# A fused attention, gating and rotation kernel: two weight transfers staged in another buffer, and one batch's attention handed out later

## The chip, the cores and the metric

The kernel runs on one core of a Trainium2 chip. The metric is the device time of the whole program in microseconds (us), as the median of several runs. TensorE (PE) does the matrix products, VectorE (DVE), ScalarE (ACT) and GpSimd (POOL) do the elementwise work, and SyncE (SP) issues nearly all DMA transfers.

## The reference, cut to what matters

```python
# B=4 batches, 8 heads, S=576 positions, 64 per head; 4 heads local (window 32), 4 strided (32)
attn = softmax(mask(q @ k.T / 8)) @ v          # heads joined: x is (B, 576, 512)
h = relu(x @ w_in)                             # 512 -> 1024
u, v = h[..., :512], h[..., 512:]
v_n = (v - mean(v)) / sqrt(var(v) + 1e-6)
v_s = einsum('ts,bsd->btd', w_spatial, v_n) + b_spatial[None, :, None]
x = (u * v_s) @ w_out
theta = x @ w_theta
y = einsum(w_tok_r, x * cos(theta)) + einsum(w_tok_i, x * sin(theta))
u2 = x + y
out = u2 + relu(u2 @ w_ch)
```

## The kernel before, in words

Every large matrix is held as two f16 halves, a high and a low part, and every product is three f16 passes (`PASS`: high x high, low x high, high x low). A weight therefore is loaded into a staging buffer, converted to its high part by ACT and to its low part by DVE or POOL, and only then read by PE. The weights `w_in`, `w_out`, `w_th`, `w_tr`, `w_ti` and `w_ch` come as 64-bit words and need four steps for each 128x1024 part: a load and two ACT activations (`a` and `b` in the hand-written list), a DVE operation (`c`), and the split into halves (`e`, ACT and POOL). The spatial weights `wsp` come as f32 and need one ACT activation and one DVE operation of 128x1152 for each of their two large parts (`sp_part(0)`, `sp_part(2)`); a third piece, `sp_tail`, holds the last rows and the bias.

There are two staging buffers, `raw0` (in tile `x2f`) and `raw1` (in tile `zf`), used in turn by `stage()`: a load into one waits until the conversion of what it held is done.

Batch 0's attention runs by itself at the start, in groups of blocks `s` = 0 to 11 (`attention0`; NG is 9). The lists in its call say what else is put between the groups: `l0`..`l3` are loads of `w_in`, `a`, `b`, `c`, `e` with the same number their conversion steps, `go` a piece of batch 0's first product with `w_in` (the half that makes v: `main_v(0)`, four times `go`), and `step` one step of batch 1's attention. Up to `pinned.clear()` each engine keeps the instructions in the order in which they are written. Batch 0's groups are written as: output transposes of group s-3 with their two evacuations into `xT[0]` (ACT high half, DVE low half), turns of group s-1, the product with V of group s-2.

After that come, for each batch, `main_v` (v), `main_mid` (u chunks, spatial chunks `sp`, products `x`, angles `th`) and `main_end` (`y` and `c`). Their instructions are no longer pinned; the tile framework's planner puts each engine's stream in order beforehand, by priorities and its own cost estimates, and at run time every engine follows its stream strictly. A count of matmul columns (`clock[0]/2400`, "clock" below, in us of TensorE at full speed) tells when to hand out other work: conversions (`conv`, by `timed(due, lead, gap)`), and steps of the next batch's attention, step n at `ATT_AT[b][0] + n*ATT_AT[b][1]`. `not_before` keeps a step's first score matmul behind the matmul that stood 3 us (`LEAD`) earlier on that clock. Since work is handed out only between chunks, a step falls on the next chunk's end.

Batch 1's attention (`attention1`) has a first step that only loads, and ten more, s = 0 to 9: scores and softmax of quad s, the transposes (`turn`) of quad s-1, the product with V (`px`) of quad s-2, whose results go to `xT[1]`. `xT[1]` is at first the place of batch 0's q and k of head pairs 2 and 3.

The names of matmul results in the profile: `at`, `sc`, `av` (banks of batch 0's groups; `av` and `sc` are also the turns and V products of batch 1), `a` (scores of batch 1), `v`, `u`, `sp`, `x`, `th`, `y`, `c`. `x2h` there is also the place of the converted 64-bit words (steps `b` and `c`), `sm` and `st` batch 1's softmax. Nearly all instructions stand on L107, the line of the helper that issues them.

Of the kernel before, what the change touches and what calls it, by code (L numbers as in the profile page):

```python
# [14 lines left out]
F32 = mybir.dt.float32  # L15
# [38 lines left out]
E_ZLO = 'vvvvvvvv'  # L54
WARM = 6
LEAD = 3.0
ATT_AT = (None, (2.7, 4.2), (86.0, 5.4), (174.5, 4.6))
PREP_AT = (112.0, 126.0, 131.0)
CONV_SP = (20.0, 9.9, 1.9)
CONV_OUT = (37.0, 12.0, 5.0)  # L60
# [9 lines left out]
def kernel(  # L70
# [52 lines left out]
    nc = Engines  # L123
# [17 lines left out]
    B, DM, S = out.shape  # L141
    P = 128
    NC = DM // P
    NF = S // P
# [61 lines left out]
    xT = [const.tile([P, 2, NC, S], F16, name=f"xT{i}") for i in range(2)]  # L206
# [10 lines left out]
    def s2(name):  # L217
        return scr.tile([P, 2, HS * 2], F32, tag="s2", name=name, bufs=4)
# [28 lines left out]
    def stage(late_raw=None):  # L247
        i = early[1]
        early[1] += 1
        if early[0]:  # L250
            return (raw0, raw1)[i % 2], vals[i % 2]
        return late_raw, s2("wx").rearrange("p a n -> p (a n)")
# [21 lines left out]
    def pair(ap, n):  # L274
        return ap[:, 0:2 * n].rearrange("p (a n) -> p a n", a=2)
# [12 lines left out]
    def prep_w(dst, src, c, i, late):  # L288
        for f in steps_w(dst, src, c, i, late):
            f()  # L290

    def win_steps(half, i):

        c = slice(half * DM, (half + 1) * DM)
        steps = []

        def load():
            steps.extend(steps_w(win, w_in, c, i, False, load_w(w_in, c, i)))

        return [load] + [lambda k=k: steps[k]() for k in range(4)]  # L300

    def sq_parts(dst, src, late=1):
        for i in range(0, NC, 2):
            yield lambda i=i: prep_w(dst, src, slice(0, DM), i, late)

    def sp_part(i):
        stg = pair(stage()[0].bitcast(F32), S)
        nc.sync.dma_start(stg, w_spT[i * P:(i + 2) * P, :].rearrange("(a p) n -> p a n", p=P))
        nc.scalar.activation(wsp[:, 0, i:i + 2, :], stg, AF.Copy, scale=SPS)
        nc.vector.scalar_tensor_tensor(wsp[:, 1, i:i + 2, :], stg, SPS, wsp[:, 0, i:i + 2, :],  # L310
                                       op0=ALU.mult, op1=ALU.subtract)
# [144 lines left out]
    NG = len(groups)  # L456
# [779 lines left out]
    def timed(parts, due, lead, gap):  # L1236
        parts = list(parts)
        for i, f in enumerate(parts):
            conv.append((due - lead - gap * (len(parts) - 1 - i), f))

    timed([lambda i=i: sp_part(i) for i in range(0, NF, 2)] + [sp_tail], *CONV_SP)
    timed(sq_parts(wout, w_out), *CONV_OUT)
    timed(sq_parts(wth, w_th), *CONV_TH)
    conv.append((conv[-1][0], switch))
# [10 lines left out]
    for at, f in [(at, lambda n=n: tok_load(*toks[n])) for n, at in enumerate(TOK_AT)] + [  # L1255
            (at, lambda: next(atts[N32])) for at in PREP_AT]:
        i = next((i for i, c in enumerate(conv) if c[0] > at), len(conv))
# [3 lines left out]
    def now():  # L1261
        return clock[0] / 2400.0

    def step():
        if next(atts[att["b"]], "end") == "end":
            att["b"] += 1
            att["n"] = 0
            return False
        att["n"] += 1
        return True  # L1270

    def others():
        while conv and conv[0][0] <= now():
            conv.pop(0)[1]()
        while att["b"] < B and ATT_AT[att["b"]][0] + att["n"] * ATT_AT[att["b"]][1] <= now():
            step()
# [13 lines left out]
    l1, a1, b1, c1, e1 = win_steps(1, 2)  # L1290
    l2, a2, b2, c2, e2 = win_steps(0, 0)
    l3, a3, b3, c3, e3 = win_steps(0, 2)
    v0 = main_v(0)

    def go():
# [6 lines left out]
        5: ((), (e0, l2)),  # L1302
        6: ((), (a1, b1)),
        7: ((), (c1, step)),
        8: ((), (e1, l3, go)),
        NG: ((), (go, step)),
        NG + 1: ((), (go, a2, b2, c2)),
        NG + 2: ((), (go, e2, a3, b3, c3, e3)),
    })
    pinned.clear()  # L1310
    run_main(v0)
# [93 lines left out]
```

## Time and profile before

| | |
|---|---|
| median of 3 runs | 489.07 us (488.37 to 489.84) |
| the profiled execution | 488.06 us, span 486.3 us |
| PE busy | 468.4 us, 96% of the span |
| DVE, ACT, POOL busy | 300.8, 267.2, 71.4 us |
[...]

The profiled execution's own time holds 1.8 us around its span. "Busy" of an engine is the time covered by its instructions; for PE the ends are modelled, so short gaps do not show.

### The profile page before, as it was taken

Reading aid. Unit: us, or ns where it says so; the run is one execution under the profiler, and the core shown is the slowest. Engines: PE = TensorE matmul, PEld = TensorE weight load, DVE = VectorE, ACT = ScalarE, POOL = GpSimd, SP = SyncE. Lnnn points to the kernel's source line nnn. Section 1 sums busy time; section 2 is a strip of 40 time slices with the busy share of each in tenths; the row PEclk is TensorE's granted clock in tenths of the full one; section 3 lists DMA queues with packets and bytes.
Section 4 is the critical chain, followed back from the end, with each engine's and each line's share of the span. In section 5 each row is a group of like instructions: output and inputs, shape, how many; then the busy total and the mean of one; then the engine's idle time right before and its main releaser. Section 6 shows DMA issues by size and latency. Waiting matters only on the chain. (4 is left out here: it accounts for less than half of the span.)

```text
span 486.3 us, 10776 instructions
## 1 busy us (share of the span) xinstructions
PE 468.4 (96%) x4440; PEld 352.3 (72%) x4440; DVE 300.8 (62%) x642; ACT 267.2 (55%) x470; POOL 71.4 (15%) x68
## 2 busy tenths in 40 slices
PE   7889889899999999999999999999999999999996
PEld 5665667676577778777568777777567777777775
DVE  3766998966998546752787878762686121227412
ACT  2657788879954334445945667754942022149202
POOL 2041124120015100201005100111005200210320
PEclk9999999999999999999999999999999999999999
DMA  6887666638760245100381345320450020003502
GB/s 179 288 243 208 201 224 217 195 154 245 161 148 1 69 163 148 54 0 1 86 217 52 91 123 158 67 44 1 74 122 1 2 98 0 1 2 76 121 0 99
DMA packets 71820, 52.72 MB, mean 108 GB/s; under 512 B 50584, under 2 KB 59992, under 8 KB 71770
## 3 DMA queue, kind: packets, MB, share of 16 engines
q1 hardware_dynamic: 71466, 51.42, 38.3%
q8 instruction: 35, 0.57, 0.5%
q10 hardware_dynamic: 304, 0.61, 0.4%
q14 instruction: 15, 0.12, 0.1%
HBM read 35.36 MB, written 4.72 MB: 82 GB/s over the span
## 5 line engine op out<-in xcount | busy, mean ns | idle before, releaser
L107 PE MATMUL y<-wtok,zf 128*128 128x288 f16 x864 | 107.2, 286 | 0.0
L107 PEld LDWEIGHTS <-zf 128*128 128x128 f16 x864 | 84.1, 98 | 22.2 <-issue 1.2
L107 PE MATMUL sp<-wsp,vn 128*128 128x288 f16 x384 | 50.3, 286 | 0.8 <-ACT u L107 0.8
L107 PE MATMUL x<-zf,wout 128*128 128x288 f16 x384 | 49.6, 287 | 0.0
L107 PE MATMUL u<-xT,win 128*128 128x288 f16 x384 | 49.3, 286 | 0.0
L107 PE MATMUL v<-win,xT 128*128 128x512 f16 (+1 forms) x240 | 48.4, 380 | 0.8 <-DVE xT L107 0.6
L107 PEld LDWEIGHTS <-vn 128*128 128x128 f16 x416 | 40.3, 98 | 11.2 <-issue 0.9
L107 PE MATMUL th<-x2h,wth 128*128 128x288 f16 x384 | 47.9, 286 | 0.3 <-DVE ta L107 0.3
L107 POOL TENSOR_TENSOR x2h<-x2f,x2h 128x576 f16<-128x576 f32 x19 | 26.6, 1403 | 142.7 <-issue 66.7
L107 PE MATMUL c<-x2h,wch 128*128 128x288 f16 x360 | 45.2, 286 | 0.0
L107 PEld LDWEIGHTS <-wth 128*128 128x128 f16 x384 | 37.6, 98 | 10.0 <-issue 0.5
L107 PEld LDWEIGHTS <-wch 128*128 128x128 f16 x384 | 37.4, 98 | 9.3
L107 PEld LDWEIGHTS <-win 128*128 128x128 f16 x384 | 37.4, 98 | 9.2
L107 PEld LDWEIGHTS <-wout 128*128 128x128 f16 x384 | 36.7, 98 | 9.5
L107 PEld LDWEIGHTS <-xT 128*128 128x128 f16 (+1 forms) x240 | 21.0, 100 | 25.3 <-issue 2.2
L107 ACT ACTIVATE x2h<-x2f 128x576 f16<-128x576 f32 (+1 forms) x28 | 20.9, 748 | 24.0 <-DVE x2f L107 23.5
L107 ACT ACTIVATE o<-c 128x576 f32<-128x576 f32 x15 | 9.7, 645 | 34.9 <-PE c L107 34.7
L107 DVE TENSOR_TENSOR ta<-ta,x2f 128x1152 f32<-128x1152 f32 (+1 forms) x17 | 21.7, 1284 | 11.2 <-ACT ta L107 11.2
L107 DVE SCALAR_TENSOR_TENSOR x2f<-y,x2f 128x576 f32<-128x576 f32 x16 | 12.1, 754 | 25.1 <-PE y L107 25.0
L107 DVE SCALAR_TENSOR_TENSOR o<-x2f,o 128x576 f32<-128x576 f32 (+1 forms) x17 | 12.2, 722 | 23.6 <-ACT o L107 23.6
L107 POOL TENSOR_TENSOR zf<-u,zf 128x576 f16<-128x576 f32 x8 | 10.2, 1277 | 112.9 <-ACT zf L107 112.9
L107 DVE TENSOR_TENSOR u<-u,sp 128x576 f32<-128x576 f32 x16 | 12.0, 750 | 22.4 <-PE sp L107 22.4
(146 smaller groups left out, 723.7 us busy)
## 6 DMA issues: line engine op xcount, KB each, us to landing
out_dram<-o SPq DMA_DIRECT2D x15, 288.0 KB
kt<-in_qp_dram SPq DMA_DIRECT2D x8, 288.0 KB
qs<-in_qd_dram SPq DMA_DIRECT2D x8, 288.0 KB
x2f<-in_w_in_dram SPq DMA_DIRECT2D x2, 1024.0 KB
zf<-in_w_in_dram SPq DMA_DIRECT2D x2, 1024.0 KB
xT<-in_w_ch_dram SPq DMA_DIRECT2D x2, 1024.0 KB
kt<-in_kzl_dram SPq DMA_DIRECT2D x8, 152.0 KB
ks<-in_kl_dram SPq DMA_DIRECT2D x4, 304.0 KB
```

Source lines behind the costliest of these rows:

```text
L107: ins = f(*args, **kwargs)
```

## The change

The two large parts of the spatial weights get a staging place of their own, the whole of `xT[1]` seen as f32. Their loads are issued with the last `w_in` load (`l3`), at group 8, and their conversions are put in the pinned list at the end of batch 0's attention, around the last `w_in` conversion; only `sp_tail` stays in `conv`. The first three conversion steps of the u half of `w_in` move one group earlier each. The second attention step of batch 1 moves from group 9 to the end of the list, and the further ones are handed out from clock 5.7 every 4.4 instead of 2.7 every 4.2. With two fewer uses of `stage()`, `sp_tail` and `w_out` still alternate as before.

```diff
-ATT_AT = (None, (2.7, 4.2), (86.0, 5.4), (174.5, 4.6))
+ATT_AT = (None, (5.7, 4.4), (86.0, 5.4), (174.5, 4.6))
...
+    raw_sp = xT[1].rearrange("p e c n -> p (e c n)").bitcast(F32)
+
+    def sp_place(i):
+        return raw_sp[:, i * S:(i + 2) * S].rearrange("p (a n) -> p a n", a=2)
+
+    def sp_load(i):
+        nc.sync.dma_start(sp_place(i), w_spT[i * P:(i + 2) * P, :].rearrange("(a p) n -> p a n", p=P))
+
     def sp_part(i):
-        stg = pair(stage()[0].bitcast(F32), S)
-        nc.sync.dma_start(stg, w_spT[i * P:(i + 2) * P, :].rearrange("(a p) n -> p a n", p=P))
+        stg = sp_place(i)
...
-    timed([lambda i=i: sp_part(i) for i in range(0, NF, 2)] + [sp_tail], *CONV_SP)
+    timed([sp_tail], *CONV_SP)
...
-        8: ((), (e1, l3, go)),
-        NG: ((), (go, step)),
-        NG + 1: ((), (go, a2, b2, c2)),
-        NG + 2: ((), (go, e2, a3, b3, c3, e3)),
+        8: ((), (e1, l3, lambda: sp_load(0), lambda: sp_load(2), go)),
+        NG: ((), (go, a2, b2, c2)),
+        NG + 1: ((), (go, e2, a3, b3)),
+        NG + 2: ((), (go, c3, lambda: sp_part(0), e3, step, lambda: sp_part(2))),
```

## Rows read from the trace of the kernel before

**Rows 1.** The page, busy time, share of the span, instructions.
```profile
PE 468.4 (96%) x4440; PEld 352.3 (72%) x4440; DVE 300.8 (62%) x642; ACT 267.2 (55%) x470; POOL 71.4 (15%) x68
```

**Rows 2.** Windows: stretch, length; busy (count) of PE, PEld, DVE, ACT, POOL; clock; DMA.
```profile
30.00:57.00 27.00, 26.14 (x260) 16.33 (x258) 19.78 (x57) 17.76 (x27) 9.60 (x9) 1.00 0.76 212
57.00:80.00 23.00, 19.47 (x230) 14.62 (x231) 22.74 (x52) 19.98 (x30) 6.36 (x6) 1.00 0.71 232
80.00:100.00 20.00, 17.46 (x230) 13.11 (x228) 17.99 (x31) 17.05 (x24) 6.63 (x6) 1.00 0.69 232
100.00:125.00 25.00, 24.68 (x219) 17.36 (x218) 15.80 (x22) 21.81 (x32) 0.00 (x0) 1.00 0.59 163
...
46.00:63.40 17.40, 15.12 (x166) 11.09 (x166) 17.24 (x51) 14.50 (x21) 2.36 (x3) 1.00 0.52 161
```

**Rows 3.** PE's waits from 0 to 100 us: total, times, longest.
```profile
PE av L107 <- DVE sm L107: 3.6, 5, 1.0
```

**Rows 4.** PE's timeline: start, length, operation, count, idle time before and its releaser.
```profile
36.01 0.73 PE L107 MATMUL a<-kt 64*64 64x96 f32 x16
...
36.85 0.51 PE L107 MATMUL av<-ident,smx 128*128 128x128 f32 x3
...
37.95 4.06 PE L107 MATMUL v<-win,xT 128*128 128x512 f16 x18
...
42.07 5.46 PE L107 MATMUL v<-win,xT 128*128 128x512 f16 x30
...
48.57 6.04 PE L107 MATMUL u<-xT,win 128*128 128x288 f16 x48
...
58.49 0.61 PE L107 MATMUL av<-ident,sm 128*96 128x128 f32 x4 [1.52 <-ACT wspt L107]
...
62.34 1.63 PE L107 MATMUL sp<-wsp,vn 128*128 128x288 f16 x12 [0.76 <-ACT u L107]
```

**Rows 5.** DVE's timeline, single operations of the stretches that the steps touch.
```profile
45.81 1.35 DVE L107 SCALAR_TENSOR_TENSOR x2h<-zf,x2h 128x1024 int32<-128x1024 int32 x1 [2.78 <-DMA x2f<-in_w_spT_dram]
...
50.63 1.48 DVE L107 SCALAR_TENSOR_TENSOR wsp<-x2f,wsp 128x1152 f16<-128x1152 f32 x1
...
52.77 1.34 DVE L107 SCALAR_TENSOR_TENSOR wsp<-zf,wsp 128x1152 f16<-128x1152 f32 x1
...
57.79 0.55 DVE L107 TENSOR_TENSOR sm<-sm,st 128x384 f32<-128x384 f32 x1
...
61.05 2.36 DVE L107 TENSOR_TENSOR vn<-vr,vn 128x1024 f16<-128x1024 f32 x2
...
84.85 0.69 DVE L107 TENSOR_TENSOR sm<-sm,st 128x512 f32<-128x512 f32 x1
...
97.48 1.29 DVE L107 TENSOR_TENSOR sm<-sm,st 128x512 f32<-128x512 f32 x1
```

**Rows 6.** ACT's timeline around the last conversions of the input weights.
```profile
38.23 0.52 ACT L107 ACTIVATE sm<-sm 128x384 f32<-128x384 f32 x1 [3.33 <-DVE sm L107]
...
42.27 0.35 ACT L107 ACTIVATE xT<-at 128x216 f16<-128x216 f32 x1 [1.13 <-PE at L107]
...
43.63 1.13 ACT L107 ACTIVATE zf<-zf 128x1024 f32<-128x1024 f32 x1
44.65 1.13 ACT L107 ACTIVATE x2h<-zf 128x1024 int32<-128x1024 uint8 x1
```

**Rows 7.** SP's timeline: when DMA transfers are issued.
```profile
33.76 0.39 SPq L107 DMA_DIRECT2D zf<-in_w_in_dram  x1
...
36.96 2.54 SPq L107 DMA_DIRECT2D v<-in_vl_dram  x4
```

**Rows 8.** SP's waits from 39.0 to 42.6 us: total, times, longest.
```profile
SPq L107 <- DMA zf<-in_w_in_dram: 1.7, 1, 1.7
```

**Rows 9.** Windows, DVE's instructions on `st` alone: the first quad's softmax.
```profile
36.90:40.30 3.40, 2.52 (x6) 1.00 1.02 341
```

**Rows 10.** POOL's timeline, one low half of an angle weight.
```profile
97.04 2.76 POOL L107 TENSOR_TENSOR wth<-x2h,wth 128x512 f16<-128x512 f32 x2 [9.88 <-ACT wth L107]
```

## Prediction

> **What bounds the kernel now.** I read the page's busy times first. PE is busy 468.4 us of 486.3 [rows 1], so a change pays only where PE stands idle, and the question is which idle time this one can reach. It starts at about 35 us, when the last groups of batch 0's attention are written; whatever comes before is the same instructions on the same engines. The windows give PE's idle time after that: from 57 to 80 us 23.00 - 19.47 = 3.53 us, from 80 to 100 us 2.54 us, from 100 to 125 us 0.32 us [rows 2]. From 36 to 57 us PE has no recorded gap. That is 6.4 us in all, 1.3% of the time, and the most that can be won.
>
> The same rows name the cause. From 46 to 63.4 us DVE is busy 17.24 of 17.40 us, from 57 to 80 us 22.74 of 23.00, while after 100 us it is busy only 63% [rows 2]. Most of PE's waits are turns of batch 1's attention that stand behind DVE's softmax (3.6 us in five waits [rows 3]), and two more are of the same kind: 1.52 us before a turn at 58.49 and 0.76 us before the first spatial product at 62.34 [rows 4]. The ACT operations named as releasers there only came at the same time: the turn reads `sm`, which DVE divided until 57.79 + 0.55 = 58.34 us, and the low half of `vn`, which the spatial product reads, was half done at 61.05 + 1.18 = 62.23 us [rows 5]. So PE waits for a DVE queue, and what counts is how much DVE work stands ahead of each thing that PE needs.
>
> **The spatial weights.** The conversions are not removed: two ACT operations and two on DVE (1.48 + 1.34 = 2.8 us [rows 5]) are moved. Before, DVE did them at 50.63 and 52.77 and was through at 54.1, eight us ahead of the first spatial product at 62.34 [rows 4, 5]. PE never waited for them, so having the weights earlier is worth nothing in itself; their worth is a place in DVE's queue that was empty. There is such a place: DVE sat idle 2.78 us before the last `c` step at 45.81 [rows 5]. (The row names a DMA; the step reads what ACT's `b3` wrote, and that ended at 44.65 + 1.13 = 45.78 [rows 6].) The loads cost SP two issues of some 0.4 us [rows 7] and DMA time behind `l3`; the loads that they delay are those of batch 1's second head pair, first read some 20 us later. I cost both at nothing; without that cover they would add up to 2 us to a quad's scores.
>
> **The step of attention moved away from group 9.** Its scores take PE from 36.01 to 36.85 us, 0.85 us [rows 4], its softmax 2.52 us of DVE [rows 9]; ACT stood idle 3.33 us for it before 38.23 [rows 6]. Without it, `a2`, `b2`, `c2` run at about 35 to 38 us and `e2` to 39.4. That sounds like a head start of 4 us for `c3`, but it is not: `a3` reads the last `w_in` part, and this load lands late. SP had issued everything by 36.96 + 2.54 = 39.50 and then waited 1.7 us for just this transfer, so it landed at 41.2 us, 7.4 us after its issue at 33.76 [rows 7, 8]. Nothing ahead of it in SP's stream changes. Before, `a3` started at 43.63 [rows 6], so this gains 2.4 us at most.
>
> **What is queued behind `a3`.** The new list writes `a3` and `b3` one group earlier, ahead of the evacuation of the last attention group (`xT`, 0.35 us on ACT, at 42.27 before [rows 6]). ACT keeps the written order, so that copy now waits for the landing at 41.2 plus the two activations, 1.02 us apart and 1.13 long [rows 6]: 41.2 + 1.02 + 1.02 = 43.25, done at 43.6, DVE's low half at 44.0. PE, with the scores gone from its stream, gets to that point 0.85 us sooner: transposes done at 42.07 - 0.85 = 41.2, then the six matmuls of the fourth `go` at 4.06/18 = 0.226 us each [rows 4], so it is through at 42.5 us. What follows (chunk 3 of v, and the scores of quad 0, whose bank the same copy has to free) needs that copy. PE stands from 42.5 to 43.65 and once more before the low half: **a new stall of 1.3 us** (0 if the load lands by 39, 1.6 if the copy loses another place). This is the first term: +1.3.
>
> [...] If ACT could reorder, the term would be 0 and the forecast 1.3 us lower.
>
> **The first spatial product.** DVE's work from the last `c` step (45.81) to the normalisation that makes `vn` is the same, with quad 0's softmax in the place of quad 1's, but starts at 44.0, behind the low half of the late copy, 1.8 us sooner; I give 0.4 back for its wait on quad 0's exponential (0.52 us on ACT [rows 6]). If quad 1's softmax, whose scores now come after the first u chunk, stays behind `vn`, the low half of `vn` is ready at 62.23 - 1.4 = 60.8 us; if it is put ahead of it, as its softmax was before, 2.5 us more: 63.3. PE starts u at about 49.2 instead of 48.57: 44.0, then the rest of v (5.46 - 1.36 = 4.1 us) and quad 0's scores, about 1.1 with their start. It has u chunks 0 to 2 (72 products at 6.04/48 = 0.126 us, 9.1 us) and two quads' scores and turns (0.85 and about 0.6 each, 2.9 us [rows 4]) before it, so arrives near 61. The stall there is 0 or about 2.2 us against 1.52 + 0.76 = 2.3 before. I take the second as nearer to the order of before, with some allowance: -0.3 (from +1.0 to -2.3).
>
> **The later turns.** Batch 1's steps come one chunk later: counted on the clock, the scores of quad k stand where those of k + 1 stood (handed out at 16.6, 19.4, 25.6, 29.0, 32.4, 37.9, 41.5, 47.3, 51.6 instead of 13.8, 16.6, 22.8, 25.6, 29.0, 32.4, 37.9, 40.8, 47.3). At any point after 63 us DVE has 2.5 us less work behind it in the queue. The stalls there were 3.53 - 2.3 + 2.54 = 3.8 us [rows 2]. Some are of the moment, a softmax behind a conversion of 1.2 to 1.4 us, and stay. The last step moves to where DVE has room. I take half: -1.9 (0 to -3.0).
>
> **The stretch after 100 us.** The work put off is added to ACT's 21.81 us busy of 25 [rows 2], where ACT also works out the angles. The stall of 0.32 us there may double: +0.3 (0 to +1.0).
>
> Sum: +1.3 - 0.3 - 1.9 + 0.3 = -0.6 us. On the profiled execution's own time of 488.06 that gives 487.5; the median shown is 1.0 us above that execution, so 488.5.
>
> **A price beside it.** DVE's multiply of 128x512 took 0.69 us alone and 1.29 us while POOL worked on a low half at 97.04 [rows 5, 10]. POOL's part of `e3` moves to about 46.4 to 48.7 us, under the spatial conversion and quad 0's multiply, so up to 2 x 0.6 = 1.2 us of the DVE queue is at risk; it lies within the bounds of the `vn` term. [...]
>
> **The rivals.** *Faster:* the DVE queue really is the bound, quad 1's softmax falls behind `vn`, and most later turns find their input. Then +1.3 - 2.2 - 2.6 + 0.3 = -3.2, 485.9 us. For it speak DVE's 99% from 46 to 80 us [rows 2]; against it the late load, which leaves DVE idle from about 40 to 43.6 us in place of the 2.78 us saved. Chance 0.34. *Slower:* both softmaxes stand ahead of `vn`. This decides as soon as `vn`'s low half comes later than about 63.5 us; then PE loses 1.3 in front, 0.9 there, keeps its later stalls and gets 0.5 after 100 us: +2.7, 491.8 us. For it speaks that DVE was already late there by 2.3 us. Chance 0.24. *The change does nothing:* the weights were ready in time anyway, and the landing sets the pace before and after, with the new stall taken back by the old: within 0.5 us of 489.07. Chance 0.06.
>
> **How the numbers follow.** My forecast, a small gain of one term over the others, has 0.36. Within 0.3% (1.5 us, about what a measurement of this kernel can tell from no change) lie the forecast and the last rival: 0.42. Faster by more 0.34, slower by more 0.24. The range reaches to both outer cases, 485.3 to 491.5; the forecast's own is 487.4 to 489.9.
>
> **What would show it.** ACT's `a3` on `zf` near 41.2 us with idle time before it; PE idle for about 1.3 us near 42.5 us, with ACT's or DVE's `xT` as releaser; the spatial conversions on DVE between 45 and 51.5 us; u from about 49.2; the spatial product at 61 to 63; fewer and shorter waits of `av` on `sm` from 63 to 100 us. Wrong would be a landing well before 41 us, no gap at 42.5, or waits from 57 to 100 us as long as before.

## The result and the profile after

The changed kernel takes 493.15 us (median of six, 492.08 to 494.6) against 488.75 us for the kernel before, measured beside it. The ratio is 1.0069 with an interval of 1.0051 to 1.0088, a loss of some 3.4 us; the two medians lie 4.4 us apart. A second set of runs of the same kernel (`after_again`, below) gave 493.04 against 488.81. The forecast of 488.5, no change to speak of, was wrong, and 493.15 lies above its range. It is also above the rival that spoke of a loss (491.8).

The page of the changed kernel, busy times and the rows of the 40 slices for PE and its granted clock:

```profile
PE 471.7 (96%) x4440; PEld 354.5 (72%) x4440; DVE 302.5 (61%) x642; ACT 267.2 (54%) x470; POOL 71.7 (15%) x68
...
PE   7789979799999999999999999999999999999996
...
PEclk9999989899999999999999999999999999999999
```

PE has the same 4440 matmuls as before [rows 1] and is busy 3.3 us longer. That is the first thing to see: PE does not wait 3.3 us more, its work takes longer. The second is in the last row: the granted clock, full in the whole span of the profiled execution before, is lower in two slices, the sixth and the eighth. The same row of the kernel before:

```profile
PEclk9999999999999999999999999999999999999999
```

To take out whatever the two executions do differently before the change, I compare the stretch from PE's first v product to its first y product. Behind it nothing differs: from y to the end it is 355.2 us before and 355.5 after. (Ahead of it the profiled execution of the changed kernel is 2.5 us later than that of the kernel before, 33.85 against 31.35, because an early load of `w_in` landed late: ACT's step on it stood idle 1.59 us and began at 18.99 instead of 16.46; in `after_again` it is 1.1 us later. The change touches nothing there, and I leave it out.) The windows of that stretch, columns as in [rows 2], first the kernel before and then the changed one:

```profile
31.35:131.09 99.74, 93.04 (x941) 63.23 (x940) 81.00 (x163) 81.90 (x117) 21.24 (x19) 1.00 0.70 205
```

```profile
33.85:137.22 103.37, 96.13 (x940) 65.15 (x939) 83.48 (x165) 84.63 (x121) 22.27 (x19) 0.97 0.66 203
```

The stretch is 3.63 us longer. PE's idle time in it went from 99.74 - 93.04 = 6.70 us to 103.37 - 96.13 = 7.24, only 0.54 more. The mean clock went from 1.00 to 0.97. Windows of a quarter of a microsecond show how: the clock is 0.50 from about 64.8 to 68.2 us and from 95.5 to 98.9, and 1.00 in the rest of the stretch. In `wait_long` (below) PE does 25 matmuls in 6 us at a clock of 0.51 and 51 at 1.00. By that each of the two stretches costs up to half its length, 1.7 us, and both up to 3.41 us. PE still stands idle in the first 0.59 and 0.29 us of them, where a low clock costs nothing; without half of that, 0.44 us, the clock costs 2.97 us, and 0.54 + 2.97 = 3.51 us stands against the 3.63 measured. The windows around the two, changed kernel:

```profile
61.00:64.00 3.00, 1.34 (x28) 0.67 (x26) 3.00 (x6) 3.00 (x4) 0.00 (x0) 1.00 0.57 172
64.00:69.00 5.00, 3.99 (x28) 2.42 (x23) 5.00 (x13) 2.90 (x5) 2.95 (x2) 0.66 0.76 260
69.00:92.00 23.00, 22.41 (x246) 17.17 (x244) 19.60 (x34) 19.50 (x28) 11.08 (x9) 1.00 0.53 192
92.00:95.00 3.00, 1.31 (x42) 0.94 (x42) 2.97 (x7) 1.89 (x3) 0.00 (x0) 1.00 0.88 207
95.00:100.00 5.00, 4.22 (x23) 3.17 (x24) 4.24 (x9) 1.72 (x4) 0.00 (x0) 0.66 0.96 349
```

Both times there is a window in which PE is busy less than half of the time (1.34 and 1.31 of 3.00 us), and behind it one with the clock at 0.66 in the mean. Between them, from 69 to 92 us, PE is busy 22.41 of 23.00 us at full clock, 97%, where before it was 85 and 87% in the stretches from 57 to 100 us [rows 2]. PE's timeline names the waits, columns as in [rows 4]:

```profile
63.00 0.42 PE L107 MATMUL sp<-wsp,vn 128*128 128x288 f16 x2 [1.55 <-ACT vn L107]
63.53 0.56 PE L107 MATMUL a<-kt 64*64 64x96 f32 x16
...
65.36 3.01 PE L107 MATMUL sp<-wsp,vn 128*128 128x288 f16 x12 [0.99 <-DVE vn L107]
...
95.78 1.09 PE L107 MATMUL av<-ident,sm 128*128 128x128 f32 x4 [2.47 <-DVE sm L107]
96.66 4.21 PE L107 MATMUL x<-zf,wout 128*128 128x288 f16 x24
```

At the first place PE waits 1.55 us for `vn`, does two spatial products and a quad's scores, and waits 0.99 us more; in that second wait the clock falls. The twelve spatial products behind it take 3.01 us, twelve took 1.63 us before [rows 4]. At the second place a turn waits 2.47 us for its softmax, the clock falls 2.2 us into the wait, and the four transposes behind it take 1.09 us (0.63 in `late_handout`, whose clock falls after them). PE's waits as a whole, 33 to 130 us, columns as in [rows 3]:

```profile
PE av L107 <- DVE sm L107: 2.5, 1, 2.5
PE sp L107 <- ACT vn L107: 1.5, 1, 1.5
PE sp L107 <- DVE vn L107: 1.1, 2, 1.0
```

Against 3.6 us in five waits of at most 1.0 before [rows 3] it is one of 2.5. The waits became fewer, as forecast, but longer, and behind the long ones PE runs at half its clock.

### The profile page after: what moved, and what is told of

It is laid out like the page before. It is cut to its first block, busy times and chain, and to the rows that moved or that the text cites. A ratio compares the mean times of both kernels' runs of the same rounds, so it can differ in the third digit from the quotient of the medians.

```text
span 492.7 us, 10773 instructions
## 1 busy us (share of the span) xinstructions
PE 471.7 (96%) x4440; PEld 354.5 (72%) x4440; DVE 302.5 (61%) x642; ACT 267.2 (54%) x470; POOL 71.7 (15%) x68
## 5 line engine op out<-in xcount | busy, mean ns | idle before, releaser
L107 PE MATMUL sp<-wsp,vn 128*128 128x288 f16 x384 | 51.5, 291 | 2.5 <-ACT vn L107 1.5
L107 PEld LDWEIGHTS <-wout 128*128 128x128 f16 x384 | 37.7, 99 | 10.7 <-issue 0.6
```

The source lines that it names most:

```text
L107: ins = f(*args, **kwargs)
```

## The experiments

The theory: idle time is much the same in both kernels, and what costs is that it is gathered into a few long waits, behind which the granted clock falls for some 3.4 us. The rivals: a cost in the change itself (the early conversions, DVE's `c` of `w_out` ahead of `vn`, the queue behind `a3`), or more waiting in all. The table has all kernels, each beside its own runs of the kernel before (488.75 to 490.28 us in the median). "v to y" is the length of the stretch above less 99.74, "idle" PE's idle time in it less 6.70, both from one profiled execution; "clock" is the sum over quarter-microsecond windows of (1 - granted clock) x length, by the same reckoning the most that the low clock can cost.

| kernel | median us | ratio (95%) | v to y | idle | clock |
|---|---|---|---|---|---|
| the changed kernel | 493.15 | 1.0069 (1.0051 to 1.0088) | +3.63 | +0.54 | 3.41 |
| after_again | 493.04 | 1.0090 (1.0072 to 1.0107) | +3.31 | +0.38 | 3.41 |
| only_attention | 493.31 | 1.0094 (1.0072 to 1.0116) | +4.39 | +1.31 | 3.41 |
| only_staging | 494.60 | 1.0108 (1.0088 to 1.0127) | +5.21 | +3.53 | 1.71 |
| staging_again | 494.78 | 1.0119 (1.0080 to 1.0159) | +6.05 | +4.12 | 1.71 |
| early_steps | 488.86 | 0.9994 (0.9978 to 1.0010) | +0.72 | +0.46 | 0 |
| earlier_steps | 493.38 | 1.0081 (1.0052 to 1.0110) | +6.07 | +1.38 | 3.41 |
| start_only | 492.50 | 1.0063 (1.0041 to 1.0084) | +1.48 | -0.63 | 1.71 |
| gap_only | 491.51 | 1.0050 (1.0032 to 1.0068) | +1.66 | +0.43 | 0 |
| late_handout | 491.38 | 1.0043 (1.0024 to 1.0063) | +4.05 | +2.09 | 1.71 |
| wout_behind_vn | 494.97 | 1.0100 (1.0064 to 1.0136) | +7.19 | +4.75 | 1.71 |
| staging_split_first | 492.59 | 1.0037 (1.0012 to 1.0063) | +4.60 | +3.02 | 1.71 |
| split_again | 492.30 | 1.0061 (1.0039 to 1.0082) | +3.59 | +2.39 | 1.71 |
| filled_first | 495.74 | 1.0123 (1.0095 to 1.0151) | +6.49 | +1.02 | 3.41 |
| filled_both | 498.95 | 1.0198 (1.0173 to 1.0222) | +6.99 | +0.42 | 1.71 |
| wait_long | 501.91 | 1.0238 (1.0202 to 1.0275) | +0.39 | +0.66 | 0 |
| wait_short | 498.83 | 1.0169 (1.0134 to 1.0203) | +0.29 | +0.55 | 0 |

Idle and clock together give "v to y" within 0.75 us except in gap_only (1.2 us short), earlier_steps (1.3 us short) and the two filled kernels, which have added work. In the last two kernels the edit lies behind this stretch. What the two columns leave over is not explained.

**The same kernel again**

> The changed kernel once more, nothing edited. Two theories of its loss. Clock: in the first trace of the changed kernel TensorE stood idle twice in front of the first spatial product (1.55 and 0.99 us) and once at a turn near 95 us (2.47 us), and its granted clock fell to 0.5 for some 4 us behind each; the waits and the half clock together make the loss. If so, the second trace shows the low clock at the same two places, and a time of about 493 us. Queue: the copy of the last attention group stands behind the two activations that wait for the last input weights, and TensorE loses 1.3 us there. If so, a gap of about 1.3 us stands near 42.5 us after the start in this trace, which the first one may have hidden, since its first part was 2.5 us late from a slow transfer near 19 us.

The two low stretches stand behind the same two waits (1.54 + 0.99 us and 2.47 us). So the low clock of the changed kernel is not an accident of one execution. The mean clock of each of its twelve executions says the same: it is 0.982 to 0.993, and none is at 1.000. The kernel before is not free of low clock either. Of its 71 executions beside the experiments, 30 have a mean clock of 1.000 (median 489.10 us) and 11 one of 0.986 to 0.993 (median 490.75 us); the full clock of its profile is the most frequent case, not a rule. Such a mean is over the whole span and does not say where the clock fell: seven of the eighteen traces have a fall that starts near 8 us, ahead of all that the change touches, and by their mean clocks lose 1.7 us or more besides what the table's last column has.

**The two halves of the change**

`only_attention`, on the kernel before: the step behind the list, and the later, wider handing out.

```diff
-        NG: ((), (go, step)),
+        NG: ((), (go,)),
...
-        NG + 2: ((), (go, e2, a3, b3, c3, e3)),
+        NG + 2: ((), (go, e2, a3, b3, c3, e3, step)),
```

> The kernel before with the attention part alone: the second attention step of batch 1 moves behind the last conversion of the input weights, and the further steps are handed out from 5.7 every 4.4; the spatial weights are staged as before. Clock theory: the attention step that is taken away is what TensorE had to do while vn was made, so this alone opens the wait before the first spatial product; 491 to 494 us, with a granted clock below 1.0 near 65 us. Queue theory: nothing stands behind the last input weights that did not before, so no loss in front; 487 to 489.5 us.

`only_staging`, on the changed kernel: handing out as before, the weights still staged early.

```diff
-ATT_AT = (None, (5.7, 4.4), (86.0, 5.4), (174.5, 4.6))
+ATT_AT = (None, (2.7, 4.2), (86.0, 5.4), (174.5, 4.6))
...
-        NG: ((), (go, a2, b2, c2)),
-        NG + 1: ((), (go, e2, a3, b3)),
-        NG + 2: ((), (go, c3, lambda: sp_part(0), e3, step, lambda: sp_part(2))),
+        NG: ((), (go, step)),
+        NG + 1: ((), (go, a2, b2, c2)),
+        NG + 2: ((), (go, e2, a3, b3, c3, lambda: sp_part(0), e3, lambda: sp_part(2))),
```

> The changed kernel with its attention put back: the lists as before and steps from 2.7 every 4.2, and only the spatial weights loaded into the second xT and converted beside the last input weights. Clock theory: TensorE has its attention work again while vn is made, so the clock stays at 1.0; the conversions fill VectorE's idle time and the time is that of before or a little less, 486.5 to 489.5 us. Queue theory: the two activations are back behind the last group's copy, so nothing is lost either; the two differ in the other runs.

The attention alone loses as much as the whole change, by two low stretches at nearly the same places, behind waits of 2.07 us (first spatial product, 61.88) and 2.13 us (a turn, 95.25). The staging alone loses in another way: +3.53 us idle. Its POOL half of `e3` runs beside a spatial conversion, which DVE does at 50.29 us. POOL's and DVE's timelines:

```profile
49.98 3.76 POOL L107 TENSOR_TENSOR win<-x2h,win 128x512 f16<-128x512 f32 x2 [4.23 <-ACT win L107]
...
50.29 1.32 DVE L107 SCALAR_TENSOR_TENSOR wsp<-xT,wsp 128x1152 f16<-128x1152 f32 x1
```

3.76 us for what took 2.28 us in the kernel before and in the changed one. It also starts 1.4 us later than before (48.62), since ACT's copy for `e3`, at 48.85, stands behind a spatial conversion, at 47.17. PE's first u product waits 2.30 us for it at 52.67, with the clock low from 52.25 to 55.75. A later turn waits 2.58 us, at full clock. Neither part is harmless, and the losses do not add up.

**The changed kernel with one number changed**

`early_steps` only sets `ATT_AT[1]` back to (2.7, 4.2); `start_only` has (5.7, 4.2), `gap_only` (2.7, 4.4), `earlier_steps` (0.0, 4.2). `late_handout` is the kernel before with (5.7, 4.4).

> The changed kernel with only the handing out put back, steps from 2.7 every 4.2; the lists stay as changed, so the input weights' two activations still stand ahead of the last group's copy. Clock theory: quad 1's scores and softmax come one chunk earlier and fill part of the wait before the first spatial product, so most of the loss is gone; 487.5 to 490.5 us. Queue theory: the loss in front stays; 491 to 494 us.

> The changed kernel with the steps handed out from 5.7, but every 4.2 as before (only the gap put back). If the later start makes the first loss (TensorE has one step less to do while vn is made), the low clock near 65 us stays and the one near 95 us may go: 490.5 to 492 us.

> The changed kernel with the steps handed out from 2.7 as before, but every 4.4 (only the start put back). If the start makes the first loss and the gap the second, the low clock near 65 us goes and the one near 95 us may stay: 488.5 to 491 us. If both stay away, the start alone is to blame.

> The kernel before with one line changed: batch 1's steps are handed out from 5.7 every 4.4. Lists, staging and the moved second step are those of before. If handing out later is what makes long waits of the many short ones, this line alone does it: one or two stretches at half clock between 60 and 100 us and 491 to 494 us. If it takes the step moved behind the list as well, the clock stays at 1.0 and the time is 488 to 490.5 us.

> The changed kernel with the steps handed out from 0.0 every 4.2, earlier than in either kernel. If later is worse because TensorE then has nothing to do while vn is made, earlier should be no worse than with 2.7: 487 to 489.5 us and no low clock; if the length of the waits goes by chance with the order that the planner finds, it may fall either way, 487 to 494 us.

With the first two numbers back, the loss is gone: 488.86 us, though the new staging, the new list and the step behind it are all there. So the early conversions and the queue behind `a3` don't make the loss by themselves. `early_steps`, v to y:

```profile
31.33:131.79 100.46, 93.30 (x940) 62.90 (x939) 79.63 (x163) 82.07 (x117) 22.83 (x19) 1.00 0.69 207
```

Its idle time, 7.16 us, is that of the changed kernel (7.24), but its longest waits are 1.84, 1.25 and 1.18 us and its clock is full. This pair is the clearest evidence for the theory: the same idle time, no low clock, 4.2 us faster. It is a pair of single traces, though. Of the twelve executions of `early_steps` four have a mean clock of 1.000 (median 488.9 us), and the six with 0.992 to 0.997 are no slower (488.7 us), so there the lower mean clock does not show in the time; where the clock fell in them is not on record.

In `start_only` the low stretch near 95 us is gone, as its expectation has it, though a turn there waits 2.70 us at full clock. The one at the first spatial product stays, behind a wait of 1.77 us. PE's timeline and a window:

```profile
62.72 0.64 PE L107 MATMUL sp<-wsp,vn 128*128 128x288 f16 x2 [1.77 <-ACT vn L107]
```

```profile
63.00:66.00 3.00, 2.85 (x28) 1.68 (x27) 3.00 (x5) 3.00 (x5) 1.77 (x2) 0.50 0.79 187
```

And the reverse, the kernel before with the later handing out alone, loses 2.3 us, with one long wait and one low stretch behind it, 97.25 to 100.75:

```profile
96.45 0.63 PE L107 MATMUL av<-ident,sm 128*128 128x128 f32 x4 [2.19 <-DVE sm L107]
```

But `earlier_steps` loses 4.3 us too (waits of 2.04 us at 93.12 and 1.99 at 121.03, a low stretch behind each). Lateness as such is therefore not the cause. Each new value of the two numbers gives another order of the engines' streams; of the five tried with the new list, four have a wait of 2 us or more somewhere, and one does not. `gap_only` is the odd one: a wait of 2.50 us at 72.03, no low clock, and still 1.8 us slower in the median; 1.2 us of its stretch stay unexplained. Its trace is of the fastest of twelve executions (490.10 us), one of two with a mean clock of 1.000. Nine have 0.986 to 0.997 (median 491.85 us), so its median holds low clock that the trace doesn't show.

**Waits made on purpose**

Seven ACT copies (`wait_long`) or two (`wait_short`) in a chain, between the first and second y product of batch 0 of the kernel before, and one small product that must read the last of them; the y product then writes over its result. PE's order is pinned for the y products of batch 0. The diff is that of `wait_long`; `wait_short` has `range(1)`.

```diff
+            if b == 0:
+                pinned.add("tensor")
+                if m == 1:
+                    g = s1("gp")[:, 0:HS]
+                    ha.activation(g, last[:, 0, 0:HS], AF.Copy)
+                    for _ in range(6):
+                        ha.activation(g, g, AF.Copy)
+                    nc.tensor.matmul(ps[:, 0, 0:P], g[:, 0:P], g[:, P:2 * P], start=True, stop=True)
+                last = ps
...
```

> The kernel before, with one wait put into a stretch where TensorE is dense and waits for nothing: between the first and the second y product of batch 0, ScalarE copies a result seven times in place and TensorE has to read the last copy (one more 128x128 matmul, overwritten at once; the output is that of before). TensorE stands idle for 3 to 3.5 us. Clock theory: behind it the granted clock is 0.5 for about 3.5 us and the products there take twice as long, so the loss is the wait plus 1.7 us: 4.5 to 5.5 us, 493.5 to 495. Idle-time rival: the loss is the wait alone, 3 to 3.5 us, and the clock stays at 1.0.

> The same with two copies: TensorE stands idle for about 1.2 us. Both theories: the clock stays at 1.0, as it did behind the waits of 1.5 and 1.8 us seen so far, and the loss is the wait, 1.0 to 1.5 us: 490 to 491.

Both waits came out longer than meant, 8.89 and 6.51 us, so the question of how short a wait can be stays unanswered by them: ACT came to the first copy late, behind conversions (at 144.83 in `wait_long`, 5.6 us into the wait). (The 1.8 us that `wait_short` takes for harmless is not always so: see `start_only`.) What they show is the price. `wait_long`, PE's timeline and windows:

```profile
148.14 0.80 PE L107 MATMUL y<-gp 128*128 128x128 f32 x2 [8.89 <-ACT gp L107]
```

```profile
148.00:154.00 6.00, 5.86 (x25) 3.91 (x26) 5.19 (x11) 2.61 (x4) 1.81 (x2) 0.51 0.01 3
154.00:160.00 6.00, 6.00 (x51) 4.79 (x50) 0.76 (x1) 0.68 (x1) 1.73 (x2) 1.00 0.00 0
```

The wait began at 139.25; the clock fell at 143.6 and came back at 153.8, 5.7 us after PE went on. In 6 us PE does 25 matmuls at 0.51 and 51 at 1.00: at half the clock half the work. From the first y product to the end it took 367.56 us against 355.19: 12.37 = 8.89 of waiting + 2.84 (half of 5.68) + 0.6. `wait_short` gives 365.60 - 355.19 = 10.41 = 6.51 + 3.1 (half of 6.2) + 0.8. In a part of the kernel that was untouched and at full clock, the clock fell behind the added wait alone, and the wait cost more than its length: 12.37 us for 8.89, and 10.41 for 6.51. These waits are for ACT; those of the changed kernel are for ACT and DVE.

**Filling the waits**

`filled_first` puts 14 matmuls of 128x512 ahead of the first spatial chunk of batch 0 in the changed kernel; `filled_both` adds 11 ahead of the turn that waited 2.47 us. They write into a bank that the next product starts anew.

```diff
+    def fill(bank, n):
+        for _ in range(n):
+            nc.tensor.matmul(bank, win[:, 0, 0, 0:P], win[:, 0, 0, 0:DM], start=True, stop=True)
...
+            if b == 0 and m == 0:
+                fill(ps[:, 0, :], 14)
...
+                bank = pa("av")
+                if b == 1 and s == 6:
+                    fill(bank, 11)
+                qd_turn(s - 1, sm, bank.rearrange("p (n k) -> p n k", n=4), pT)
```

> The changed kernel with 14 extra matmuls of 128x512 (3.0 us) written into the bank of the first spatial product just ahead of it; their results are overwritten, nothing else is computed otherwise. They stand in the two waits for vn (1.55 + 0.99 us). Clock theory: TensorE is busy there, the granted clock stays at 1.0 near 65 us, and the 3.5 us at half clock, worth up to 1.75 us, come back; the time is 491 to 492 us though the kernel does 3 us more work. Rival, that the idle time alone makes the loss: the extra work can win nothing, and what of it does not fit the waits is lost; 493 to 494 us.

> The same, and 11 more extra matmuls of 128x512 (2.3 us) into the bank of the turns, ahead of the turn that stood idle for 2.47 us near 95 us. Clock theory: no low clock at either place; 3.5 us come back, less what does not fit: 489 to 490.5 us. Idle-time rival: 493 us or more. The planner gives the streams behind the first place another order, so the second place counts less than the first.

As a means to a faster kernel this failed: both are slower. They do 3.0 and 5.3 us more work, and the order that came out has a new wait of 2.1 us on the next turn (65.98 and 67.52 us), where the clock falls instead; so the first place tests nothing. The second place is a test of the cause. PE's timeline and windows there, first `filled_first`, where it is not filled, then `filled_both`:

```profile
96.65 1.09 PE L107 MATMUL av<-ident,sm 128*128 128x128 f32 x4 [2.43 <-DVE sm L107]
97.53 3.31 PE L107 MATMUL x<-zf,wout 128*128 128x288 f16 x17
```

```profile
97.00:102.00 5.00, 5.00 (x86) 3.68 (x85) 2.03 (x5) 2.14 (x4) 0.00 (x0) 0.73 0.49 182
```

```profile
94.71 2.55 PE L107 MATMUL av<-win 128*128 128x512 f16 x11
...
98.14 0.63 PE L107 MATMUL av<-ident,sm 128*128 128x128 f32 x4 [0.88 <-DVE sm L107]
98.60 3.10 PE L107 MATMUL x<-zf,wout 128*128 128x288 f16 x24
```

```profile
98.00:103.00 5.00, 4.86 (x95) 4.01 (x95) 3.03 (x7) 3.83 (x5) 0.00 (x0) 1.00 0.22 64
```

With PE kept at work through most of the wait the clock stayed full, 1.00 from 98 to 103 us where it was 0.73 from 97 to 102: the same transposes take 0.63 instead of 1.09 us, and 24 products 3.10 us where 17 took 3.31. It is one trace of each kernel, and a wait of this length does not bring the clock down every time (below). `filled_both` is nevertheless 3.2 us slower than `filled_first`; 1.8 us of that lie behind y, where nothing was changed, and are not explained.

**DVE's queue ahead of `vn`, and the order of the conversions**

`wout_behind_vn` keeps the `c` steps of `w_out` and later weights behind the low half of `vn`, by an ordering dependency. `staging_split_first` is `only_staging` with `e3` ahead of both spatial parts.

```diff
-        NG + 2: ((), (go, e2, a3, b3, c3, lambda: sp_part(0), e3, lambda: sp_part(2))),
+        NG + 2: ((), (go, e2, a3, b3, c3, e3, lambda: sp_part(0), lambda: sp_part(2))),
```

> The changed kernel with VectorE's operation of each later 64-bit conversion kept behind the low half of batch 0's vn; nothing else is fixed. In the changed kernel the first of w_out (1.22 us) stands right ahead of vn's low half, since its load now lands earlier. If that is what makes the second wait before the spatial product (0.99 us), it goes, and with it perhaps the low clock near 64 us, worth 1.75 us more: 490.3 to 492. If the wait for the high half (1.55 us) alone lowers the clock, only the 1 us or less comes back: 492 to 493.

> The run with the staging alone, with both spatial conversions written behind the last split of the input weights (e3) and not around it. There, ScalarE's copy for e3 stood behind a spatial one, and GpSimd's low half took 3.76 us in place of 2.28 beside VectorE's conversion; TensorE waited 2.30 us for it and ran at half clock for 3.5 us. If that was the loss, both go: 489.5 to 491.5 us. If the loss lies in the spatial conversions' place ahead of vn, it stays near 494.

> The run with the staging alone once more. In its first trace a wait of 2.58 us near 80 us left the clock at 1.0, while one of the same length in the run with the split first was followed by half clock. If the low clock goes by the instructions alone, this trace shows the same again: low near 52 us, not near 80. If it also depends on what the chip did in the microseconds before, it may be low near 80 us here. Time as before, 493 to 495 us.

> The run with the split first once more. By the instructions alone: low near 79 us again and nowhere else between 30 and 130 us, 490.5 to 493 us. If the low clock comes and goes from run to run at the same wait, the times spread by 1.7 us, as they did here (490.4 to 494.1).

The first made it worse: the wait before the first spatial product shrinks to 0.56 us and no low clock stands there, but a turn just ahead of it waits 1.53 us, and behind one of 3.29 us at 97.64 the clock falls, the 1.71 us of the table. It also shows the stall that I had forecast, at 44.63, 1.57 us, released by `xT`. The second removes the 2.30 us before u as meant (2.30 and 2.31 us in `only_staging` and `staging_again`, none in the two splits), and is some 2 us faster than `only_staging`, but still slower than the kernel before, and above the 489.5 to 491.5 us expected.

The two repeats bring out what the theory can't say. In `staging_again` and `split_again` the same turn waits the same 2.60 us and the same instructions follow. PE's timeline of `staging_again`, then of `split_again`:

```profile
80.86 0.61 PE L107 MATMUL av<-ident,sm 128*96 128x128 f32 x4 [2.60 <-DVE sm L107]
...
82.27 0.69 PE L107 MATMUL sc<-pT,v 96*64 96x64 f32 x16
82.89 0.56 PE L107 MATMUL a<-kt 64*64 64x64 f32 x18
```

```profile
78.15 0.61 PE L107 MATMUL av<-ident,sm 128*96 128x128 f32 x4 [2.60 <-DVE sm L107]
...
79.64 1.12 PE L107 MATMUL sc<-pT,v 96*64 96x64 f32 x16
80.69 0.90 PE L107 MATMUL a<-kt 64*64 64x64 f32 x18
```

In the first the clock stays at 1.00; in the second it is 0.50 from 79.25 to 83.0, and the rows show its price at either level: 1.12 against 0.69 us and 0.90 against 0.56 for the same matmuls. In the first traces of the two kernels it came out the same way (the wait 2.58 us both times). But that holds for the traced executions only. Five of the nine executions of `split_again`, and three of the twelve of `staging_split_first`, have a mean clock of 1.000 over the whole span, so no fall at all. These eight took 490.89 to 492.32 us (median 491.5), the other thirteen 490.39 to 494.05 us (median 492.9). The low clock thus comes and goes between executions of one kernel, and those with it are some 1.4 us slower in the median. `start_only` too has a wait of 2.70 us at full clock, and `wait_long` one of 2.21 us in the part that is that of the kernel before:

```profile
93.98 0.63 PE L107 MATMUL av<-ident,sm 128*128 128x128 f32 x4 [2.21 <-DVE sm L107]
```

So neither the length of a wait nor the order of the instructions decides by itself; what does is open.

No version beat the kernel before.

## Why the prediction was wrong, point by point

**The bound.** Right as far as it went: PE's idle time from 35 us on is the only thing that the change reaches, and it comes from DVE's queue. What was missing is that the time lost to a wait can be more than its length (12.37 us for 8.89 in `wait_long`), and this is the step that failed: every term prices a wait at its length alone. I read the full clock of the page and of every window [rows 2] as a given, and no term, bound or rival priced its loss; it was put at nothing without a reason. The two stretches of 3.4 us at half clock cost 3.0 to 3.4 us: nearly the whole loss, where the idle time made 0.54 us.

**The spatial weights.** That they are worth nothing in themselves agrees with `early_steps`, which has them and is within 0.1 us of the kernel before. Only the first found the place meant for it; the forecast had both between 45 and 51.5 us. DVE's timeline of the changed kernel:

```profile
46.55 1.35 DVE L107 SCALAR_TENSOR_TENSOR wsp<-xT,wsp 128x1152 f16<-128x1152 f32 x1
...
54.27 1.34 DVE L107 SCALAR_TENSOR_TENSOR wsp<-xT,wsp 128x1152 f16<-128x1152 f32 x1
```

**The new stall, +1.3 us.** The mechanism is there, its size not. ACT's timeline of the changed kernel, columns as in [rows 6]:

```profile
42.69 1.15 ACT L107 ACTIVATE zf<-zf 128x1024 f32<-128x1024 f32 x1 [0.88 <-DMA zf<-in_w_in_dram]
...
44.76 0.33 ACT L107 ACTIVATE xT<-at 128x216 f16<-128x216 f32 x1
```

`a3` waits for the landing, 0.88 us, and the copy stands behind `b3`, as forecast. That ACT does not take the copy ahead of its turn is plainest in `wout_behind_vn`: PE's transposes for it were done at 41.38 + 0.38 = 41.76 us, ACT stood idle until `a3` at 42.21, and the copy came behind `b3`, at 44.25. But in the changed kernel v had begun 2.5 us later than before, so set against v the load landed a microsecond sooner than in the sum, and PE did not wait for the copy. No gap there was one of the prediction's own signs of being wrong. The stall goes with the time from v's first product to `a3`, which the sum had at 41.2 - 31.35 = 9.85 us. It is 8.84 us in the changed kernel, 8.45 in `after_again` and 8.58 in `gap_only`, without a stall; 9.44 us in `early_steps`, with a stall of 0.61 us; and 10.37 us in `wout_behind_vn`, with one of 1.57 us. PE's timeline of these last two:

```profile
43.23 0.60 PE L107 MATMUL v<-win,xT 128*128 128x512 f16 x2 [0.61 <-ACT xT L107]
```

```profile
44.63 0.61 PE L107 MATMUL v<-win,xT 128*128 128x512 f16 x2 [1.57 <-ACT xT L107]
```

The term was within its bounds (0 to 1.6), and moves with a transfer that the change does not touch.

**The first spatial product, -0.3 us.** PE waited 1.55 + 0.99 = 2.54 us there against 2.28, so +0.3: a miss, within the bounds of +1.0 to -2.3. For the second of the two waits, that for the low half, DVE's timeline says why, columns as in [rows 5]:

```profile
61.82 1.22 DVE L107 SCALAR_TENSOR_TENSOR x2h<-zf,x2h 128x1024 int32<-128x1024 int32 x1
62.95 2.35 DVE L107 TENSOR_TENSOR vn<-vr,vn 128x1024 f16<-128x1024 f32 x2
```

With the spatial weights out of the staging buffers, `w_out` is loaded sooner, and its `c` step stands ahead of `vn`'s low half; before, it came behind it, at 64.79. The longer wait, for the high half, stays unexplained by this, and `wout_behind_vn`, where the `c` step is out of the way, still has 1.53 + 0.56 us of waiting there. I had asked which softmax would stand there and not what the freed buffers would bring forward.

**The later turns, -1.9 us.** This term was off by 1.2 us, about as much as the new stall. "I take half" rested on 2.5 us less DVE work in the queue. Between the first spatial products and 100 us PE waited 0.44 us (a product `x` on POOL's `zf`) and 2.47 us (a turn), 2.91 in all against 3.64 in five waits of 0.49 to 0.99 before, so -0.7 in place of -1.9, within the bounds of 0 to -3.0. The last turns moved past 100 us, and the next term takes that back. Fewer waits, as forecast, but one of them as long as three had been. The DVE rows ahead of it:

```profile
90.88 1.24 DVE L107 TENSOR_TENSOR wtok<-wx,wtok 128x576 f16<-128x576 f32 x1
...
92.78 1.35 DVE L107 SCALAR_TENSOR_TENSOR wx<-zf,wx 128x1152 int32<-128x1152 int32 x1
94.05 0.75 DVE L107 TENSOR_TENSOR zf<-u,zf 128x576 f16<-128x576 f32 x1
...
94.94 0.69 DVE L107 TENSOR_TENSOR sm<-sm,st 128x512 f32<-128x512 f32 x1
```

The softmax that the turn needs is cut into small operations, and conversions of 1.2 to 1.4 us stand between them. I had named this ("some are of the moment, and stay") and yet halved the sum. And, against the silent assumption that a wait costs its length, this one cost 2.47 us and up to 1.7 us more.

**The stretch after 100 us, +0.3 us.** PE waited 0.90 and 0.24 us there, 1.14 against 0.32 [rows 2]: +0.8, within the bounds. Waits alone thus sum to +0.3 - 0.7 + 0.8 = +0.4 us, where the forecast had +1.3 - 0.3 - 1.9 + 0.3 = -0.6. With that alone the forecast would have been one microsecond off; the clock made it more than four.

**The rivals.** The slower one had the right sign by another mechanism: it counted the idle time alone, and idle time is +0.5 us. Its 491.8 also lay outside the range of 485.3 to 491.5, which was said to reach to both outer cases. None of the rivals was what happened.

**What is left open.** The first ratio gives 3.4 us, that of `after_again` 4.4 us; the stretch has 3.3 to 3.6 us, and the further microsecond of the second ratio and of the medians has no place in the traces. That half the clock makes most of the loss is shown by the two traces and by the clocks of all twelve executions. That the clock falls behind a wait for another engine is shown by the waits made on purpose, 8.89 and 6.51 us, about three times as long as those of the changed kernel. At this kernel's own lengths it is argued, from `filled_both` at its second place and from `early_steps` beside the changed kernel, whose order differs in more than the waits. Which waits of 1.8 to 2.7 us do it and which don't is not known.

## What to carry to other kernels

In a kernel whose PE is busy 95% of the time, don't add up the waits alone: look at the longest of them and at the granted clock behind each, and price a wait of about 2 us at its length plus a possible 1.7 us, half of the 3.4 us at 0.50 seen here. A change can leave the sum of the waits nearly as it is and still lose by gathering them (7.24 us of idle time here against 7.16 in `early_steps`, and over 4 us between the medians), so after any change of the order of work read the clock first, in narrow windows, and not the page's average (0.992 here), and compare the mean clock of several executions before a fall in one trace is put down to the order of work. And when a buffer is freed, ask which transfer starts sooner for it and which engine's queue its conversion will then stand in.

## What the runs showed of the hardware that was not expected

- The granted clock fell to 0.50 for about 3.4 us behind waits of 1.77 to 3.29 us for another engine, and once in the second of two waits of 1.55 and 0.99 us with 1.4 us of small products between them (PE worked about 1.4 us of 3.9). Waits of 1.84, 2.21, 2.50, 2.58, 2.60 and 2.70 us in other kernels left it at 1.00, and some executions of one and the same kernel show a fall and others none.
- It need not fall in the wait: in the changed kernel it fell 2.2 us into a wait of 2.47, in `split_again` 1.3 us after one of 2.60, when PE was at work again. It came back 3.4 us after its fall in all those cases, but 10.2 us after it in `wait_long`, 5.7 us after PE went on.
- POOL's low half of an input weight took 3.76 us in `only_staging`, where DVE did a conversion of 128x1152 in the same time (1.32 us, at 50.29), and 3.76 us again in `staging_again`; it took 2.28 us in the changed kernel, where that conversion lies ahead of it but for 0.1 us, and in `staging_split_first`, where it comes behind it but for 0.3 us. That the one slows the other was not tried by itself.
